# Attention with joined tanh and joined exponentials, ahead of a gated and a three-branch feed-forward, on one core

## The chip, the cores and the metric

The kernel runs on one core of a Trainium2 chip. The metric is the device time of one execution in microseconds (us). The engines are named as the profile names them: PE multiplies matrices (PEld is its loading of weights, which overlaps), ACT is ScalarE, DVE VectorE, POOL GpSimd, and SP issues the DMAs. SBUF is the on-chip memory of 128 partitions; PSUM has eight banks of 512 float32 columns per partition, into which PE writes.

## The reference, cut to what matters

Three stages follow each other; all inputs and outputs are float32.

```python
# q, k, v: (2, 12, 448, 64); cap = 30
scores = (q @ k.T) / sqrt(64)
scores = cap * tanh(scores / cap)
attn   = softmax(scores)            # guard 1e-9 in the sum
x      = (attn @ v) as (896, 768)

h = x @ w_in                        # 768 -> 2048
g = P(h) / (Q(h) + 1e-6)            # P cubic, Q = 1 + |b0||h| + |b1|h^2
x = g @ w_out                       # 2048 -> 768

h = max(x @ w1, x @ w2, x @ w3)     # 768 -> 768 each
out = h @ w_out2                    # 768 -> 768
```

## The kernel before, in words

**Attention.** The 24 heads of the two batches are 12 pairs of heads, and two pairs make a group `d` (six groups, `B * ND`). The 448 keys are three chunks of 128 (`NFULL` = 3) and a short rest of 64. `scores(d, i)` (line 566) makes one score value of a group: for i from 0 to 5, pair `r = i // 3` and chunk `n = i % 3`, and for i = 6 the rests of both pairs. Such a value is 128 keys by 448 queries for two heads and takes two PSUM banks, one per head (`singles`, line 334; `pair`, line 358). On it run
- PE: `products` (line 578, four instructions; mode "rows") or `ends` (line 585, eight; mode "both"),
- ACT: `soft` (line 599), one tanh of 448 columns per head out of its bank, with `1/(8 cap)` as a scale in a one-column tensor,
- ACT: `expo` (line 602), one exponential over the 896 columns of both heads in SBUF, in place, with `cap` as a scale. The reference's maximum is not subtracted: the scores are bounded by `cap`.

The result `E[d, i]` lies in a slot of its own. `weighted_rest(d)` (line 619) multiplies the rest's exponentials with v, and `weighted(d, r)` (line 638, twelve instructions) those of the three chunks of a pair, two times six halves, into a bank. The softmax's sums come from `summed(d)`: for the first three groups (`ADDED`) DVE or POOL add the three chunks of a pair first (line 660), and PE then sums over the keys with ones (line 684, 16 instructions); for the last three groups PE sums all chunks (32 instructions). The sums go out of their bank (line 695) through DRAM for reshaping and reciprocals and return as rows that scale the product (`scale_pair`, line 714), which is then split into a high and a low part (lines 730 and 734).

**Weights.** They come as float64 bits into three `raw` buffers and are decoded to float32 by ACT or POOL and DVE (lines 419 to 442) and split into a high and a low part (lines 459 and 462); a weight takes a slot while it is decoded and two for its parts. This goes on beside attention. The feed-forward stages then run on PE without a pause: `up` (line 754), `down` (line 861), the products of the three branches by a 2x2 scheme with seven products (line 998), and `output` (line 1106).

**What sets the order.** No engine's order is written out. Each operation is entered by `add` with its cost per engine that can run it, what it follows, and what memory it holds. `Flow.issue` (line 170) then plays the program through time, operation by operation: PE's operations carry due times from the order in which the program enters them, the others get theirs from those that need them, and each engine takes the earliest due that is ready and finds its memory. Costs of all engines but PE and SP are multiplied by `SPARE` (line 47, 1.08), and PE pays `SWITCH` for a change of mode (line 46). Operations marked `shared` go to whichever engine is free sooner by the plan. What the plan puts on an engine stays in that order on the chip.

**Memory.** 51 slots (`NSLOT`) of 2 x 448 columns hold everything in SBUF except constants, `raw` buffers and rows. `place` (line 113) gives a score value one of the pairs of banks (0, 1), (2, 3) and, for the first five groups (`EARLY`), also (6, 7): the pair that has been free the longest. As long as scores are to come, sums and products of attention use banks 4 and 5; after the last score all eight banks serve every kind.

Of the kernel before, what the change touches and what calls it, by code (L numbers as in the profile page):

```python
# [8 lines left out]
F32 = mybir.dt.float32  # L9
# [20 lines left out]
CAP = 6  # L30
NG = 6
LAG = 3
NSLOT, NRAW, NROW = 51, 3, 4
ND = NPAIR // 2
NFULL = S // P
WARM = 3
# [7 lines left out]
BACKLOG = 14.0, 2.0  # L44

SWITCH, SAME = {"rows": 0.21, "both": 0.16, "halves": 0.16, "quarters": 0.13, None: 0.2}, 6.0
SPARE = 1.08

MM, MO, FULL = 0.206, 0.1733, 0.752

# [29 lines left out]
class Flow:  # L80
# [6 lines left out]
    def __init__(self, pools, make):  # L87
        self.make = make
        self.ops, self.clock, self.free = [], 0.0, {k: list(range(n)) for k, n in pools.items()}
        self.banks, self.freed, self.log = [None] * 8, [0.0] * 8, []  # L90
        self.idle, self.t = {}, 0.0

    def add(self, engines, fn, after=(), vals=(), shared=False, due=None, leave=0, ahead=1e9, size=0.0, mode=None):
        first = next(iter(engines))
# [75 lines left out]
    def issue(self):  # L170
# [6 lines left out]
            assert op.due is not None, op.fn  # L177
        order = [op for op in ops if "pe" in op.engines]
        self.scores = sum(any(v.kind == "sc" for v in op.vals) for op in order)
        names = ("pe", "act", "dve", "pool", "sp")  # L180
        busy = dict.fromkeys(names, 0.0)
        current = dict.fromkeys(names)
# [8 lines left out]
        while left:  # L191
# [81 lines left out]
            while events and events[0][0] <= t + 1e-9:  # L273
                _, _, op = heapq.heappop(events)
                if op is None:
                    continue
                for v in op.vals:
                    v.users -= 1
                    if not v.users:
                        if v.kind in self.free:  # L280
                            self.free[v.kind].append(v.at[0])
                            if v.kind == "raw":
                                self.idle[v.at[0]] = t
                                seq += 1
                                heapq.heappush(events, (t + REST, seq, None))
                        else:
                            for i in v.at:
                                self.banks[i], self.freed[i] = None, t
                if any(v.kind == "sc" for v in op.vals) and "pe" in op.engines:
                    self.scores -= 1  # L290
                for s in op.next:
                    s.left -= 1
                    s.ready = max(s.ready, op.done + self.CROSS)
                    if not s.left:
                        k = len(ready)
                        while k and ready[k - 1].due > s.due:
                            k -= 1
                        ready.insert(k, s)
                        if s.ready > t:
                            seq += 1  # L300
                            heapq.heappush(events, (s.ready, seq, None))
# [8 lines left out]
def attention_moe(ctx: ExitStack, tc: tile.TileContext, qk, v, w_in, w_out, w123, w_out2, par, out):  # L310
# [6 lines left out]
    def open_pool(name, **kw):  # L317
        return ctx.enter_context(tc.tile_pool(name=name, bufs=1, reuse_waits="tile", **kw))

    cp = open_pool("consts")  # L320
    sp = open_pool("slots")
    pp = open_pool("banks", space=PSUM)
    dr = ctx.enter_context(tc.tile_pool(name="scratch", bufs=1, space=DRAM))


# [5 lines left out]
    ones = cp.tile([P, 3, Q], F32, name="ones")  # L331
    raws = [sp.tile([P, DM, 2], I32, name=f"raw{i}") for i in range(NRAW)]
    rows = [sp.tile([P, S], F32, name=f"row{i}") for i in range(NROW)]
    singles = [pp.tile([P, 512], F32, name=f"b{i}") for i in range(8)]
    a0, a1, a2, a3 = (con[:, i : i + 1] for i in range(4))
    b0, b1 = absb[:, 0:1], absb[:, 1:2]
    cap = con[:, CAP : CAP + 1]

    def make(val):
        if val.kind == "s":  # L340
            val.tile = sp.tile([P, 2, S], val.dt, tag=f"s{val.at[0]}", bufs=1, name=val.name)

    fl = Flow({"s": NSLOT, "raw": NRAW, "row": NROW}, make)
    add = fl.add

    def slot(name, dt=F32):
# [9 lines left out]
        return singles[val.at[0]]  # L356

    def pair(val, j):
        return singles[val.at[j]]

    def dma(out_, in_, after=(), vals=(), size=0.0, issue=0.4, **kw):
        return add({"sp": issue}, lambda e: nc.sync.dma_start(out=out_(), in_=in_()), after, vals, size=size, **kw)
# [197 lines left out]
        at = 2 * S - 2 * D + j * D  # L560
        return flat(vr, 2 * S)[r * D : r * D + D, at : at + D]

    last_tanh, last_copy = [], []


    def scores(d, i):
        whole_ = i < 2 * NFULL
        r, n = divmod(i, NFULL)
        pis = [2 * d + r] if whole_ else [2 * d, 2 * d + 1]
        t, x = Val("sc", f"sc{d}_{i}"), slot(f"e{d}_{i}")  # L570
        t.early = d < EARLY

        def products(e):
            raw = QK[pis[0]][0]
            q, k = two(raw)[:, 0], two(raw)[:, 1, n * P : n * P + P]
            for j in range(2):
                rr = slice(j * D, j * D + D)
                pe.matmul(pair(t, j)[:, :S], k[rr], q[rr], start=True, stop=True)  # L578

        def ends(e):  # L580
            for h, pi in enumerate(pis):
                raw = QK[pi][0]
                for j in range(2):
                    rr = slice(j * D, j * D + D)
                    pe.matmul(
                        pair(t, j)[h * D : h * D + D, :S], two(raw)[rr, 1, NFULL * P :], two(raw)[rr, 0],
                        start=True, stop=True,
                    )

        done = add(  # L590
            {"pe": FULL}, products if whole_ else ends, [QK[pi][1] for pi in pis], [QK[pi][0] for pi in pis] + [t],
            mode="rows" if whole_ else "both",
        )
        for th in last_tanh[-2:]:
            th.before(done)

        def soft(e):
            for j in range(2):
                act.activation(two(x)[:, j], pair(t, j)[:, :S], AF.Tanh, scale=qscale)  # L599

        def expo(e):
            act.activation(two(x), two(x), AF.Exp, scale=cap)  # L602

        th = add({"act": 1.03}, soft, [done, scale_in], [t, x])
        last_tanh.append(th)
        E[d, i] = x, add({"act": 0.935}, expo, [th], [x])

    AV, XU = {}, {}

# [1 line left out]
    def weighted_rest(d):  # L611
        vr, got_v = VV[d]
        o = [Val("av", f"av{d}_{r}") for r in range(2)]
        x, ex = E[d, 2 * NFULL]

        def products(e):
            for r in range(2):
                for j in range(2):
                    pe.matmul(  # L619
                        bank(o[r])[j * D : j * D + D, :S], rest(vr, r, j), two(x)[r * D : r * D + D, j],  # L620
                        start=True, stop=False,
                    )

        done = add({"pe": FULL}, products, [ex, got_v], [*o, x, vr], mode="both")
        AV[d] = o, done
        XU[d] = slot(f"xu{d}"), []
        for c in last_copy[-2:]:
            c.before(done)

    def weighted(d, r):  # L630
        vr, got_v = VV[d]
        o, dep = AV[d][0][r], AV[d][1]
        es = [E[d, r * NFULL + n] for n in range(NFULL)]

        def products(e):
            for n, (x, _) in enumerate(es):
                for j in range(2):
                    pe.matmul(  # L638
                        bank(o)[j * D : j * D + D, :S], whole(vr, n, r, j), two(x)[:, j], start=False,
                        stop=n == NFULL - 1,  # L640
                    )

        dep = add(
            {"pe": NFULL * FULL}, products, [got_v, dep] + [ex for _, ex in es], [o, vr] + [x for x, _ in es],
            mode="halves",
        )
        xu, parts = XU[d]
        parts.append(add(
            {"dve": 0.54, "act": 0.43}, lambda e: copy_on[e](two(xu)[:, r], bank(o)[:, :S]), [dep], [o, xu]
        ))  # L650
# [3 lines left out]
    def added(d, r):  # L654
        y, done = slot(f"es{d}_{r}"), None
        for n in range(ADDED[d]):
            (x, ex), (z, ez) = (E[d, r * NFULL] if n == 0 else (y, done)), E[d, r * NFULL + n + 1]

            def plus(e, x=x, z=z):
                engine[e].tensor_tensor(out=two(y), in0=two(x), in1=two(z), op=ALU.add)  # L660

            done = add({"dve": 1.0, "pool": 2.1}, plus, [ex, ez, done], [x, y, z], shared=True)
        ADDS[d, r] = y, done

    def summed(d):
        if ADDED[d]:
# [11 lines left out]
        def products(e):  # L678
            for n in range(last + 1):
                for r in range(2):  # L680
                    x = rounds[r][n][0]
                    for j in range(2):
                        g = (2 * r + j) * Q
                        pe.matmul(  # L684
                            bank(t)[g : g + Q, :S], ones[:, 0 if n < last else 1 + r], two(x)[:, j], start=n == 0,
                            stop=n == last, tile_position=(0, g),
                        )

        es = rounds[0] + rounds[1]
        dep = add(  # L690
            {"pe": (last + 1) * FULL}, products, [ex for _, ex in es] + [filled], [t] + [x for x, _ in es],
            mode="quarters",
        )
        got = add(
# [486 lines left out]
```

## Time and profile before

| | |
|---|---|
| median of the timed runs | 495.18 us (three runs, 495.1 to 497.91) |
| the profiled execution | 500.3 us |
| its span, first to last instruction | 498.5 us |
| PE busy | 492.1 us, 99% |
| DVE busy | 425.6 us, 85% |
| ACT busy | 335.5 us, 67% |
| POOL busy | 93.4 us, 19% |
| tanh, line 599 | 84 instructions of 128x448 |
| exponential, line 602 | 42 instructions of 128x896 |

All numbers of the trace are from the one profiled execution. Busy time of PE counts pipelined matrix multiplications with modelled ends, so a full PE row does not by itself mean that PE never waited; starts of instructions and the list of waits tell that.

### The profile page before, as it was taken

To read this page: it belongs to the slowest core of one execution; us is meant where nothing else is said; L and a number is where in the kernel's file an instruction comes from. 1 tells how busy PE (TensorE), PEld (TensorE's weight loads), DVE (VectorE), ACT (ScalarE), POOL (GpSimd) and SP (SyncE) were. 2 spreads that over 40 slices of the span, in tenths; PEclk is the share of its full clock that TensorE was granted. 3 is DMA by queue.
4 is the path that set the end of the run, shared out by engine and by line. 5 is a ranking of instruction groups with operands and counts; after the bars stand their busy time and mean duration, and the time that the engine had idled before them with its cause. 6 is when DMAs were issued, how large, how long until landed. Compare 5 with 4: busy or idle time off the path is not lost.

```text
span 498.5 us, 6724 instructions
## 1 busy us (share of the span) xinstructions
PE 492.1 (99%) x2508; PEld 400.8 (80%) x2508; DVE 425.6 (85%) x605; ACT 335.5 (67%) x443; POOL 93.4 (19%) x78
## 2 busy tenths in 40 slices
PE   8999999999999999999999999999999999999997
PEld 4432333479899999999999999999999999999996
DVE  0499999899999989989999999789999999989200
ACT  4999999978768878876586856574625454663211
POOL 0222223113311030220001000152223213102000
PEclk9999999999999999999999999999999999999999
DMA  7956545655000010311112576403235043220211
GB/s 285 411 201 240 165 156 158 221 143 188 2 0 1 0 64 1 126 65 63 65 42 85 192 252 215 165 0 128 83 114 183 2 141 111 84 107 1 96 64 63
DMA packets 16448, 58.36 MB, mean 117 GB/s; under 512 B 3592, under 2 KB 6944, under 8 KB 16416
## 3 DMA queue, kind: packets, MB, share of 16 engines
q1 hardware_dynamic: 16416, 57.94, 33.4%
q8 instruction: 19, 0.31, 0.3%
q14 instruction: 13, 0.11, 0.1%
HBM read 55.10 MB, written 2.84 MB: 116 GB/s over the span
## 4 chain that ended last, share of the span: by engine, by line
PE 86%; DVE 5%; ACT 4%; DMA 2%; issue 1%; SPq 0%; DVEq 0%
PE b L861 24%; PE b L998 24%; PE b L754 19%; PE b L1106 9%; PE b L578 4%; PE b L638 4%; PE b L684 3%; ACT e L599 2%; DVE es L660 2%; DMA raw<-in_w_out_dram 2%; DMA qk<-in_qk_dram 1%; PE b L619 1%; DVE decin L442 1%; DVE decin L423 1%; ACT e L602 1%
## 5 line engine op out<-in xcount | busy, mean ns | idle before, releaser
L754 PE MATMUL b<-x,whin 128*128 128x448 f32 x384 | 109.7, 367 | 0.0
L754 PEld LDWEIGHTS b<-x,whin 128*128 128x128 f32 x384 | 71.8, 188 | 8.3 <-issue 2.1
L754 PE MATMUL b<-x,wlin 128*128 128x448 f32 x192 | 70.1, 365 | 0.0
L998 PE MATMUL b<-T,mh 128*128 128x448 f32 x216 | 62.0, 368 | 0.0
L439 ACT ACTIVATE raw<-raw 128x768 uint8<-128x768 uint8 x30 | 58.1, 1974 | 0.1
L599 ACT ACTIVATE e<-b,qscale 128x448 f32<-128x448 f32 x84 | 47.7, 732 | 3.8 <-PE b L578 3.7
L998 PEld LDWEIGHTS b<-T,mh 128*128 128x128 f32 x216 | 40.5, 188 | 4.0
L602 ACT ACTIVATE e<-e,con 128x896 f32<-128x896 f32 x42 | 43.4, 1158 | 0.0
L998 PE MATMUL b<-T,ml 128*128 128x448 f32 x108 | 39.7, 368 | 0.0
L793 POOL TENSOR_TENSOR T<-T,A 128x448 f32<-128x448 f32 x16 | 23.9, 1493 | 82.6 <-ACT T L778 61.1
L754 PEld LDWEIGHTS b<-x,wlin 128*128 128x128 f32 x192 | 36.1, 188 | 2.9
L578 PE MATMUL b<-qk 64*128 64x448 f32 x144 | 36.5, 604 | 0.7 <-DMA qk<-in_qk_dram 0.7
L774 ACT ACTIVATE W<-b,con 128x448 f32<-128x448 f32 x32 | 23.1, 723 | 19.2 <-PE b L754 19.1
L861 PE MATMUL b<-gl,whoa 128*128 128x448 f32 x96 | 35.2, 367 | 0.5 <-DVE gl L836 0.5
L861 PE MATMUL b<-gh,whob 128*128 128x448 f32 x96 | 35.3, 368 | 0.0
L861 PE MATMUL b<-gl,whob 128*128 128x448 f32 x96 | 35.3, 368 | 0.0
L861 PE MATMUL b<-gh,wlob 128*128 128x448 f32 x96 | 35.3, 368 | 0.0
L861 PE MATMUL b<-gh,wloa 128*128 128x448 f32 x96 | 35.1, 365 | 0.0
L861 PE MATMUL b<-gh,whoa 128*128 128x448 f32 x96 | 35.1, 365 | 0.0
L419 POOL TENSOR_SCALAR decin<-raw 128x768 f32<-128x768 f32 x15 | 19.0, 1267 | 80.5 <-DMA raw<-in_w_in_dram 38.1
L578 PEld LDWEIGHTS b<-qk 64*128 64x128 f32 x144 | 15.7, 197 | 20.2 <-ACT e L599 9.7
L998 PE MATMUL b<-B,mh 128*128 128x448 f32 x108 | 31.0, 368 | 0.0
(157 smaller groups left out, 1132.3 us busy)
## 6 DMA issues: line engine op xcount, KB each, us to landing
raw<-in_w_out_dram SPq DMA_DIRECT2D x22, 768.0 KB, 4.2
raw<-in_w_dram SPq DMA_DIRECT2D x18, 768.0 KB, 4.3
raw<-in_w_in_dram SPq DMA_DIRECT2D x16, 768.0 KB, 5.1
qk<-in_qk_dram SPq DMA_DIRECT2D x12, 448.0 KB, 7.4
v<-in_v_dram SPq DMA_DIRECT2D x6, 448.0 KB, 6.0
row<-rsum SPq DMA_DIRECT2D x24, 112.0 KB, 2.9
out_dram<-ob SPq DMA_DIRECT2D x6, 384.0 KB, 2.7
out_dram<-ob SPq DMA_DIRECT2D x2, 192.0 KB, 1.9
```

The lines of the kernel that those rows point to most:

```text
L419: engine[e].tensor_scalar(out=o, in0=i, scalar1=2.0**-112, scalar2=0.0, op0=ALU.mult, op1=ALU.add)
L439: act.activation(byte[:, 4::8], byte[:, 3::8], AF.Copy, scale=1 / 32, bias=-31 / 64)
L578: pe.matmul(pair(t, j)[:, :S], k[rr], q[rr], start=True, stop=True)
L599: act.activation(two(x)[:, j], pair(t, j)[:, :S], AF.Tanh, scale=qscale)
L602: act.activation(two(x), two(x), AF.Exp, scale=cap)
L638: pe.matmul(bank(o)[j * D : j * D + D, :S], whole(vr, n, r, j), two(x)[:, j], start=False, stop=n == NFULL - 1,)
L754: pe.matmul(bank(h)[:, :S], w_, x_, start=cc == 0 and i == 0, stop=cc == NCC - 1 and i == len(terms) - 1)
L774: act.activation(two(w_)[:, i], bank(h)[:, :S], AF.Identity, bias=a2, scale=a3)
L793: engine[e].tensor_tensor(out=two(t_)[:, i], in0=two(t_)[:, i], in1=two(a_)[:, i], op=ALU.mult)
L861: pe.matmul(bank(a)[:, :S], w_, g_, start=count[half, o, b] == 1, stop=count[half, o, b] == 3 * NFC)
L998: pe.matmul(bank(o)[:, :S], w_, m_, start=cc == 0 and i == 0, stop=cc == 2 and i == 2)
L1106: pe.matmul(bank(o)[:, :NH], h_, w_, start=ocs[0] == 0 and i == 0, stop=ocs[-1] == NCC - 1 and i == len(terms) - 1,)
```

## The change

Banks 0 to 3 become two tiles of two banks each (`twins`) as long as scores are to come. A score value that lies in one of them gets its tanh by one instruction over both banks; one in banks 6 and 7 still takes two. The three chunks of a pair of heads share one tile of SBUF, a triple (`tri`, four of them, `NTRI`, kind "t"), and one exponential over its 2688 columns follows the third tanh. The rest of the keys keeps a slot and an exponential of its own. Twelve of the 51 slots are held back for the triples and return to the slots when the last triple is released; the two pools are closed at that point and at the first later use of a bank below 4, and pools for single slots and banks are opened in their place. In the plan, a tanh in a two-bank tile costs 0.89 and any other 1.03, the long exponential 0.187 + 3 x 0.747, and `SPARE` is 1.06.

```diff
-NSLOT, NRAW, NROW = 51, 3, 4
+NSLOT, NRAW, NROW, NTRI = 51, 3, 4, 4
...
-SPARE = 1.08
+SPARE = 1.06
+
+TANH = 0.89
...
         self.idle, self.t = {}, 0.0
+        self.held = 3 * pools["t"]
+        self.late, self.free["s"] = self.free["s"][len(self.free["s"]) - self.held :], self.free["s"][: -self.held]
...
                             self.free[v.kind].append(v.at[0])
+                            if v.kind == "t":
+                                self.triples -= 1
+                                if not self.triples:
+                                    self.free["s"] += self.late
...
-    singles = [pp.tile([P, 512], F32, name=f"b{i}") for i in range(8)]
+    singles = [None] * 4 + [pp.tile([P, 512], F32, name=f"b{i}") for i in range(4, 8)]
+    tri = triples_open.enter_context(tc.tile_pool(name="triples", bufs=1, reuse_waits="tile"))
+    pairs = pairs_open.enter_context(tc.tile_pool(name="pairs", bufs=1, reuse_waits="tile", space=PSUM))
+    twins = [pairs.tile([P, 2, 512], F32, name=f"bb{i}") for i in range(2)]
...
     def make(val):
+        at = val.at[0]
+        if val.kind == "t":
+            val.tile = tri.tile([P, NFULL, 2, S], val.dt, tag=f"t{at}", bufs=1, name=val.name)
         if val.kind == "s":
-            val.tile = sp.tile([P, 2, S], val.dt, tag=f"s{val.at[0]}", bufs=1, name=val.name)
+            if at >= NSLOT - 3 * NTRI and not late:
+                triples_open.close()
+                late.append(open_pool("late"))
+            pool = late[0] if at >= NSLOT - 3 * NTRI else sp
+            val.tile = pool.tile([P, 2, S], val.dt, tag=f"s{at}", bufs=1, name=val.name)
+        if val.kind in ("h", "acc", "av") and at < 4 and singles[0] is None:
+            pairs_open.close()
+            more = open_pool("more", space=PSUM)
+            singles[:4] = [more.tile([P, 512], F32, name=f"b{i}") for i in range(4)]
...
     def pair(val, j):
-        return singles[val.at[j]]
+        at = val.at[j]
+        return twins[at // 2][:, at % 2] if at < 4 else singles[at]
...
-        t, x = Val("sc", f"sc{d}_{i}"), slot(f"e{d}_{i}")
+        t = Val("sc", f"sc{d}_{i}")
         t.early = d < EARLY
+        if not whole_:
+            x = slot(f"e{d}_{i}")
+            view = lambda: two(x)
+        else:
+            if not n:
+                TRI[d, r] = Val("t", f"e{d}_{r}"), []
+            x, parts = TRI[d, r]
+            view = lambda: x.tile[:, n]
...
         def soft(e):
+            if t.at[0] < 4:
+                act.activation(view(), twins[t.at[0] // 2][:, :, :S], AF.Tanh, scale=qscale)
+                return
             for j in range(2):
-                act.activation(two(x)[:, j], pair(t, j)[:, :S], AF.Tanh, scale=qscale)
+                act.activation(view()[:, j], pair(t, j)[:, :S], AF.Tanh, scale=qscale)
 
         def expo(e):
-            act.activation(two(x), two(x), AF.Exp, scale=cap)
+            all_ = two(x) if not whole_ else x.tile.rearrange("p n j s -> p (n j s)")
+            act.activation(all_, all_, AF.Exp, scale=cap)
 
-        th = add({"act": 1.03}, soft, [done, scale_in], [t, x])
+        th = add({"act": TANH}, soft, [done, scale_in], [t, x])
         last_tanh.append(th)
-        E[d, i] = x, add({"act": 0.935}, expo, [th], [x])
+        if not whole_:
+            E[d, i] = x, add({"act": 0.935}, expo, [th], [x]), view
+            return
+        parts.append(th)
+        if n == NFULL - 1:
+            ex = add({"act": 0.187 + 0.747 * NFULL}, expo, parts, [x])
+            for k in range(NFULL):
+                E[d, r * NFULL + k] = x, ex, lambda k=k: x.tile[:, k]
```

The rest of the diff passes the views of `E` on to the products, additions and sums that read them, counts the triples, and sets the planned cost of a tanh by the banks that its score has got.

## Rows read from the trace of the kernel before

**Rows 1.** Waits of PE: who waited for whom, us in total, times, longest.

```profile
PE b L861 <- DVE gl L836: 0.5, 1, 0.5
PE b L684 <- DVE es L660: 0.4, 1, 0.4
```

**Rows 2.** Chain that ended last, from 46 us on: start us, us, what.

```profile
46.07 1.70 PE b L684 x12
47.77 2.46 PE b L578 x12
...
51.89 2.41 PE b L638 x12
54.29 1.70 PE b L578 x8
...
60.86 1.64 PE b L684 x16
...
87.39 3.14 PE b L684 x32
...
103.09 3.86 PE b L754 x18
```

**Rows 3.** Stretches: length, busy PE, PEld, DVE, ACT, POOL, clock, DMA, GB/s.

```profile
10.57:47.70 37.13, 36.68 (x195) 13.46 (x193) 28.43 (x34) 37.02 (x59) 9.27 (x8) 1.00 0.80 307
47.70:103.02 55.32, 55.32 (x350) 21.00 (x348) 53.83 (x85) 52.82 (x76) 14.40 (x10) 1.00 0.52 166
103.02:131.01 27.99, 27.52 (x136) 24.83 (x134) 25.83 (x38) 22.23 (x30) 5.53 (x5) 1.00 0.41 131
```

**Rows 4.** Timeline of PE, 12 to 45 us: start us, us, engine, line, what.

```profile
12.27 7.99 PE L578 MATMUL b<-qk 64*128 64x448 f32 x32
20.19 0.98 PE L619 MATMUL b<-e,v 64*64 64x448 f32 x8
...
27.07 2.81 PE L638 MATMUL b<-e,v 128*64 128x448 f32 x12
29.81 3.27 PE L578 MATMUL b<-qk 64*128 64x448 f32 x12
33.01 0.96 PE L684 MATMUL b<-es,ones 128*32 128x448 f32 x8
...
36.35 1.72 PE L619 MATMUL b<-e,v 64*64 64x448 f32 x8
38.00 2.48 PE L638 MATMUL b<-e,v 128*64 128x448 f32 x12
...
44.68 0.95 PE L684 MATMUL b<-es,ones 128*32 128x448 f32 x4
```

**Rows 5.** Timeline of PE's weight loads, with the idle time before and its releaser.

```profile
37.10 0.20 PEld L619 LDWEIGHTS b<-e,v 64*64 64x64 f32 x4 [0.56 <-DVE row L695]
```

**Rows 6.** Timeline of ACT, 7 to 32 us.

```profile
7.69 1.16 ACT L599 ACTIVATE e<-b,qscale 128x448 f32<-128x448 f32 x2 [2.99 <-PE b L578]
...
10.68 8.52 ACT L599 ACTIVATE e<-b,qscale 128x448 f32<-128x448 f32 x16 [0.33 <-PE b L578]
18.97 1.15 ACT L602 ACTIVATE e<-e,con 128x896 f32<-128x896 f32 x1
19.90 2.33 ACT L599 ACTIVATE e<-b,qscale 128x448 f32<-128x448 f32 x4
...
28.60 3.40 ACT L599 ACTIVATE e<-b,qscale 128x448 f32<-128x448 f32 x6
```

**Rows 7.** Groups of ACT by line and shape: count, busy us, mean ns of one.

```profile
L459 ACT CAST mh<-decm 128x768 fp32r<-128x768 f32 x15 | 12.6, 840 | 8.0 <-DVE decm L432 4.6 <-PE b L998 2.2 <-DVE decm L490 1.1
...
L459 ACT CAST mx<-decm 128x384 fp32r<-128x384 f32 x9 | 4.7, 523 | 10.9 <-DVE decm L490 3.9 <-PE b L998 3.3 <-DVE ml L462 2.8
```

**Rows 8.** Groups of DVE by line, operations on a weight.

```profile
L462 DVE TENSOR_TENSOR wlin<-decin,whin 128x768 fp32r<-128x768 f32 x16 | 16.2, 1014 | 0.0
L432 DVE SCALAR_TENSOR_TENSOR decin<-raw,decin 128x768 int32<-128x768 int32 x16 | 15.9, 996 | 0.3
```

More of the change, by code (lines that the diff above doesn't have):

```diff
@@ L179, in issue @@
         self.scores = sum(any(v.kind == "sc" for v in op.vals) for op in order)
+        self.triples = len({id(v) for op in ops for v in op.vals if v.kind == "t"})
         names = ("pe", "act", "dve", "pool", "sp")
@@ L322, in attention_moe @@
     pp = open_pool("banks", space=PSUM)
+    pairs_open, triples_open = ExitStack(), ExitStack()
+    ctx.enter_context(triples_open)
+    ctx.enter_context(pairs_open)
     dr = ctx.enter_context(tc.tile_pool(name="scratch", bufs=1, space=DRAM))
@@ L337, in attention_moe @@
     cap = con[:, CAP : CAP + 1]
+    late = []
     def make(val):
+        at = val.at[0]
+        if val.kind == "t":
+            val.tile = tri.tile([P, NFULL, 2, S], val.dt, tag=f"t{at}", bufs=1, name=val.name)
         if val.kind == "s":
-            val.tile = sp.tile([P, 2, S], val.dt, tag=f"s{val.at[0]}", bufs=1, name=val.name)
-    fl = Flow({"s": NSLOT, "raw": NRAW, "row": NROW}, make)
+            if at >= NSLOT - 3 * NTRI and not late:
[7 more added lines that the diff above has]
+            singles[:4] = [more.tile([P, 512], F32, name=f"b{i}") for i in range(4)]
+    fl = Flow({"s": NSLOT, "raw": NRAW, "row": NROW, "t": NTRI}, make)
     add = fl.add
@@ L561, in rest @@
         return flat(vr, 2 * S)[r * D : r * D + D, at : at + D]
-    last_tanh, last_copy = [], []
+    last_tanh, last_copy, TRI = [], [], {}
     def scores(d, i):
@@ L575, in products @@
             q, k = two(raw)[:, 0], two(raw)[:, 1, n * P : n * P + P]
+            th.engines["act"] = (TANH if t.at[0] < 4 else 1.03) * SPARE
             for j in range(2):
@@ L580, in ends @@
         def ends(e):
+            th.engines["act"] = (TANH if t.at[0] < 4 else 1.03) * SPARE
             for h, pi in enumerate(pis):
@@ L613, in weighted_rest @@
         o = [Val("av", f"av{d}_{r}") for r in range(2)]
-        x, ex = E[d, 2 * NFULL]
+        x, ex, view = E[d, 2 * NFULL]
         def products(e):
@@ L619, in products @@
                     pe.matmul(
-                        bank(o[r])[j * D : j * D + D, :S], rest(vr, r, j), two(x)[r * D : r * D + D, j],
+                        bank(o[r])[j * D : j * D + D, :S], rest(vr, r, j), view()[r * D : r * D + D, j],
                         start=True, stop=False,
@@ L635, in products @@
         def products(e):
-            for n, (x, _) in enumerate(es):
+            for n, (_, _, view) in enumerate(es):
                 for j in range(2):
                     pe.matmul(
-                        bank(o)[j * D : j * D + D, :S], whole(vr, n, r, j), two(x)[:, j], start=False,
+                        bank(o)[j * D : j * D + D, :S], whole(vr, n, r, j), view()[:, j], start=False,
                         stop=n == NFULL - 1,
@@ L643, in weighted @@
         dep = add(
-            {"pe": NFULL * FULL}, products, [got_v, dep] + [ex for _, ex in es], [o, vr] + [x for x, _ in es],
+            {"pe": NFULL * FULL}, products, [got_v, dep] + [ex for _, ex, _ in es], [o, vr] + [x for x, _, _ in es],
             mode="halves",
@@ L656, in added, with plus @@
         for n in range(ADDED[d]):
-            (x, ex), (z, ez) = (E[d, r * NFULL] if n == 0 else (y, done)), E[d, r * NFULL + n + 1]
-            def plus(e, x=x, z=z):
-                engine[e].tensor_tensor(out=two(y), in0=two(x), in1=two(z), op=ALU.add)
+            (x, ex, one), (z, ez, other) = (E[d, r * NFULL] if n == 0 else (y, done, lambda: two(y))), E[d, r * NFULL + n + 1]
+            def plus(e, one=one, other=other):
+                engine[e].tensor_tensor(out=two(y), in0=one(), in1=other(), op=ALU.add)
             done = add({"dve": 1.0, "pool": 2.1}, plus, [ex, ez, done], [x, y, z], shared=True)
-        ADDS[d, r] = y, done
+        ADDS[d, r] = y, done, lambda: two(y)
     def summed(d):
@@ L680, in products @@
                 for r in range(2):
-                    x = rounds[r][n][0]
+                    x = rounds[r][n][2]()
                     for j in range(2):
@@ L684, in products @@
                         pe.matmul(
-                            bank(t)[g : g + Q, :S], ones[:, 0 if n < last else 1 + r], two(x)[:, j], start=n == 0,
+                            bank(t)[g : g + Q, :S], ones[:, 0 if n < last else 1 + r], x[:, j], start=n == 0,
                             stop=n == last, tile_position=(0, g),
@@ L690, in summed @@
         dep = add(
-            {"pe": (last + 1) * FULL}, products, [ex for _, ex in es] + [filled], [t] + [x for x, _ in es],
+            {"pe": (last + 1) * FULL}, products, [ex for _, ex, _ in es] + [filled], [t] + [x for x, _, _ in es],
             mode="quarters",
```

## The prediction

> **What bounds the kernel now.** I read four views in this order. First the list of waits of the matrix engine (PE): behind 47.7 us of the span it holds one wait, 0.5 us [rows 1]. So the later 450 us are PE work without a hole, and what the change can give back has to be found ahead of that point. Second, the chain that ended last: from 46.07 to 106.95 us it is 30 PE pieces, each beginning where the one before it ends [rows 2]. From the same rows come the full-rate prices: three score operations (x12) take 2.46 us and two (x8) 1.70, so one costs 0.76 and the change of mode about 0.2; a weighted product (x12) costs 2.41 and a row sum of the first kind (x16) 1.64. Third, the engines by stretch: from 10.57 to 47.7 us ScalarE (ACT) is busy 37.02 of 37.13 us, while VectorE (DVE) is busy 28.43; from 47.7 to 103.02 us ACT, DVE and PE are all nearly full (52.82, 53.83 and 55.32 of 55.32) [rows 3]. Early on ACT sets the pace, later PE does, with DVE close behind it.
>
> Fourth, PE's timeline of the early stretch gives the idle time by subtraction [rows 4]:
> - 12.27 to 20.19 us: eight scores take 7.92; at full rate 8 x 0.76 + 0.2 = 6.28. Idle 1.64; ACT's tanh paces them.
> - 20.19 to 29.81 us: two operations on the short rest of the keys, then a score and a weighted product twice, take 9.62; at full rate, with 0.16 for a change of mode, 2 x 0.92 + 2 x (0.92 + 2.41) = 8.50. Idle 1.12; the products follow the exponentials.
> - 29.81 to 33.01 us: three scores take 3.20 against 2.46. Idle 0.74; tanh again.
> - 36.35 to 38.00 us: one product of the short rest takes 1.65 against 0.92. Idle 0.73; it waits for DVE's copy of a row sum out of its bank [rows 5].
> - 44.68 to 47.77 us: a row sum takes 3.09 against 1.64. Idle 1.45; it waits for DVE's additions (the second wait in rows 1).
>
> Together 5.68 us: 3.50 behind ACT and 2.18 behind DVE. Whatever ACT saves, the end can move by little more than this.
>
> **The change, part by part.**
>
> *One tanh over two banks.* Sixteen single tanhs run from 10.68 to 18.97 us [rows 6], 0.518 us each, and two are a score's: 1.036. No row shows one instruction that reads two banks. What an ACT element costs comes from two casts: 840 ns for 768 columns, 523 for 384 [rows 7], so 317 / 384 = 0.826 ns a column and 0.370 us for 448. That leaves 0.148 us fixed per tanh, which the joined one pays once: 0.888 us, 0.148 saved. The other end comes from the kernel's own pair: tanh on 448 columns 0.518, exponential on 896 0.93 (18.97 to 19.90) [rows 6], or 0.92 ns a column and 0.106 fixed, 0.106 saved. Lowest of all, crossing from bank to bank eats the whole saving: 0. A loss is left out, because the same columns are read with one start fewer. I take 0.148, since the two casts differ in size alone. A score lies in banks 0 to 3 in two of three cases for the first five groups of heads (35 scores, three pairs of banks) and always in the last group (7 scores): about 23 + 7 = 30. Saved: 30 x 0.148 = 4.4 us of ACT.
>
> *One exponential for three chunks.* An exponential costs 0.93, of which 2 x 0.370 = 0.740 are columns and 0.19 fixed. Three in one: 0.19 + 3 x 0.740 = 2.41 against 2.79, so 0.38 saved, twelve times: 4.6 us. With 0.106 fixed it is 0.21 x 12 = 2.5. Both parts: 9.0 us of ACT, at the low end 2.5 (no gain from the joined tanh).
>
> The Trainium skill, ScalarE: Activation LUTs, section on the ACT_TABLE_LOAD cost ("What ACT_TABLE_LOAD costs"), gives an ACTIVATE with one pointer operand about 280 ns plus 0.833 ns a column, with an overlap of about 93 ns back to back. By that an estimate for the single tanh is 0.56 us, which the trace has at 0.518, and for the exponential 0.93, which the trace has too. It would make the saving of a joined tanh 0.19 instead of 0.148 and ACT's total about 10 us instead of 9.0.
>
> *What of it reaches the end.* By 28.60 us ACT has done 26 tanhs (13 scores, some 8.7 of them joined) and two triples of exponentials [rows 6]: 8.7 x 0.148 + 2 x 0.38 = 2.05 us ahead. Against it stands a loss. Now a weighted product runs behind its exponentials chunk by chunk: the second one starts at 27.07, before the third exponential ends at 28.60, and PE goes on at 29.81, 1.21 us after that end. With one exponential it can start only at its end and needs 2.41: 1.20 us of overlap gone. Net at 29.81: 2.05 - 1.20 = 0.85 us. The three scores behind it then find their banks emptied and run in 2.46 instead of 3.20: 0.74 more, 1.6 us at 33.01. The loss of overlap does not return: from 38.00 us on the weighted products run at full rate (x12 in 2.41), their exponentials done before. At 44.68 ACT is further ahead (23 scores, four triples: 15.3 x 0.148 + 4 x 0.38 = 3.8 us), so DVE's additions get their inputs earlier, but DVE's own queue stands between. Of the 2.18 us behind DVE I take 0.9: at worst none goes, at best all. Sum: 1.6 + 0.9 = 2.5 us. With ACT's savings at their low end the first part is 2 x 0.21 - 1.20 + 0.74 = 0, and with some of the second about 0.5 remain.
>
> *After 47.7 us* ACT's remaining 5 us of savings lie beside full PE work and move nothing. They cover something else, though: PE now comes 2.5 us earlier to everything, and DVE has 1.5 us free until 103.02 and 2.2 until 131.01 [rows 3]. The planner lets ACT take over casts and copies where DVE is behind, and I cost this at nothing on that cover. Without it, PE's lead would be paid back, up to 2.5 us.
>
> *Tiles and planner.* Four triples hold 12 of the 51 slots all through attention, where before each chunk took its slot and gave it back alone. Two groups of heads need all four triples, so the next group's first tanh waits until the oldest group's weighted products and additions, and from the fourth group on its row sum, are done. In the program's order these stand ahead of the next group's scores, so I cost this at nothing, with ACT's lead as cover; the upper bound is a row sum, 1.64 or 3.14 us [rows 2], for each of the four groups to which it can happen. Closing the pools issues no work; the first users of banks 0 to 3 wait for the last joined tanh as before for the last single one. SPARE 1.06 for 1.08 and the new costs reorder everything that is planned by time; with about 0.2 us for each change of PE's mode [rows 2], five more or fewer are 1 us either way.
>
> The profiled execution took 500.3 us, its span 498.5; the median of the timed runs is 495.18. The 2.5 us are taken off both: 497.8 for a profiled run, 492.7 for the median.
>
> **The rivals.**
> 1. *DVE holds the pace, nothing comes.* The joined operations close later and may come too late for DVE's additions; or the two-bank tanh saves nothing, so that the change does not do what it says. Then the 0.5 us of the low end remain at most: 494.7 to 495.2. For it: DVE ends the last early wait. Against it: 3.50 of the 5.68 us are behind ACT.
> 2. *All early idle goes.* Order and inputs fall so that neither ACT nor DVE keeps PE waiting: 495.18 - 5.7 = 489.5. For it: ACT's lead of 3.8 us by then; against it: the 1.20 us of lost overlap and DVE's queue.
> 3. *Slower: the slots that the triples keep.* Two triples fall idle when the fifth group's row sum ends (about 90.5 us), but their six slots go to nobody until the last weighted product ends at 103.09 [rows 2]. That is room for two decoded weights (three slots each). Of each, DVE does two operations of 0.996 us (one has a row, the other the same shape) and one of 1.014 [rows 8], 3.0 us, so 6.0 us of DVE work slip to a time when 2.2 us are free until 131 us. 6.0 - 2.2 = 3.8 us, and PE's lead of 2.5 us makes them come later still in its own time: 6.3 late, 495.18 - 2.5 + 6.3 = 499.0. It decides from the point at which more than 4.7 us (2.2 and the lead) slip. For it: DVE is 97% busy there. Against it: no wait in the trace names a lack of room, and ACT gets spare time in just this stretch.
>
> **How the numbers follow.** Forecast, 1 to 4.5 us gained: 0.60. Rival 1, within 1 us: 0.17. Rival 2, more than 4.5: 0.11. Rival 3 and other disorder from the new plan, slower: 0.12. The range reaches to rival 2 with a us for fewer mode changes (488.5) and to near rival 3 (498.0). 1% is 4.95 us, about what a measurement of this kernel can tell from no change: over it on the fast side lies most of rival 2 and a little of the forecast's upper end, 0.13; on the slow side the worse half of rival 3, 0.07; between, 0.80.
>
> **What would show it.** Right: tanhs of 896 columns at 0.89 us from start to start, some 30 of them; twelve exponentials of 2688 columns at 2.4; ACT's attention ends some 9 us earlier or has other work between; PE's idle time ahead of its unbroken run is about 3 us instead of 5.7, and that run begins correspondingly earlier. Wrong: PE waits of over 1 us behind 50 us of the span, on decoded weights or on DVE (rival 3); the row sums of the first groups still waiting for DVE's additions at the same time as before (rival 1); a joined tanh at 1.03 us.

## The result and the profile after

The changed kernel takes 492.08 us in the median of 20 runs, against 496.0 us for the kernel before in 20 runs beside it: a ratio of 0.9917, with a 95% interval of 0.9896 to 0.9938, so some 4 us faster (3 to 5). The forecast was 492.7 us.

The profile on which the prediction rests comes from one of the longer executions (nine of the 20 runs before took 497 us or more, one of the 20 after 494 us or more; the fastest are 494.70 and 491.62 us), in which PE ran its first scores at half rate and its products from about 280 us on 2% slower, so a second profile of the same kernel (run before_again) is the one to compare with here. First lines of the two pages, after and before:

```profile
span 490.4 us, 6637 instructions
PE 482.6 (98%) x2508; PEld 399.1 (81%) x2508; DVE 415.2 (85%) x596; ACT 337.2 (69%) x402; POOL 91.8 (19%) x73
```

```profile
span 492.7 us, 6724 instructions
PE 487.0 (99%) x2508; PEld 400.3 (81%) x2508; DVE 425.9 (86%) x605; ACT 335.0 (68%) x443; POOL 96.2 (20%) x78
```

The spans differ by 2.3 us, a little less than the medians. ACT has 41 instructions less, yet no less busy time: it took over work from DVE and POOL. What the joined instructions cost is in ACT's groups, after and then before_again (count, busy us, mean ns of one); line 638 is the joined tanh, 641 the single one, 645 the exponential:

```profile
L638 ACT ACTIVATE e<-bb,qscale 128x896 f32<-128x896 f32 x31 | 31.4, 1069 | 3.4 <-PE bb L616 3.0 <-PE b L734 0.5
L645 ACT ACTIVATE e<-e,con 128x2688 f32<-128x2688 f32 x12 | 31.3, 2608 | 0.1
...
L641 ACT ACTIVATE e<-b,qscale 128x448 f32<-128x448 f32 x22 | 13.5, 705 | 0.0
...
L645 ACT ACTIVATE e<-e,con 128x896 f32<-128x896 f32 x6 | 6.9, 1146 | 0.0
```

```profile
L599 ACT ACTIVATE e<-b,qscale 128x448 f32<-128x448 f32 x84 | 47.7, 748 | 2.4 <-PE b L578 2.4
L602 ACT ACTIVATE e<-e,con 128x896 f32<-128x896 f32 x42 | 43.7, 1171 | 0.0
```

Before they are 91.4 us together, after 83.1: 8.3 us saved of the 9.0 forecast, with 31 joined tanhs for the 30 expected. From start to start a joined tanh takes 0.89 us and a long exponential 2.43 (19.77 to 22.20), as ACT's timeline after shows. The separate last line is from before_again and is the tanh that follows the second pair's three exponentials there:

```profile
9.00 1.92 ACT L638 ACTIVATE e<-bb,qscale 128x896 f32<-128x896 f32 x2
10.78 1.19 ACT L641 ACTIVATE e<-b,qscale 128x448 f32<-128x448 f32 x2
...
19.77 2.62 ACT L645 ACTIVATE e<-e,con 128x2688 f32<-128x2688 f32 x1
22.20 1.99 ACT L638 ACTIVATE e<-bb,qscale 128x896 f32<-128x896 f32 x2
```

```profile
26.14 3.44 ACT L599 ACTIVATE e<-b,qscale 128x448 f32<-128x448 f32 x6
```

Where the time came from stands in PE's timeline. First after (line 616 scores, 688 weighted products, 734 row sums), then before_again, which answers to [rows 4]; both begin their first score at 5.1 us:

```profile
5.11 1.77 PE L616 MATMUL bb<-qk 64*128 64x448 f32 x8
...
18.22 2.48 PE L688 MATMUL b<-e,v 128*64 128x448 f32 x12 [1.45 <-ACT e L645]
...
24.85 1.77 PE L616 MATMUL bb<-qk 64*128 64x448 f32 x8
...
28.07 0.96 PE L734 MATMUL b<-es,ones 128*32 128x448 f32 x8
...
30.44 1.02 PE L616 MATMUL bb<-qk 64*128 64x448 f32 x4 [0.66 <-ACT e L638]
31.39 1.38 PE L669 MATMUL b<-e,v 64*64 64x448 f32 x6
...
40.94 0.96 PE L734 MATMUL b<-es,ones 128*32 128x448 f32 x8
...
42.59 1.78 PE L616 MATMUL bb<-qk 64*128 64x448 f32 x8
```

```profile
5.09 2.53 PE L578 MATMUL b<-qk 64*128 64x448 f32 x12
...
27.38 3.27 PE L578 MATMUL b<-qk 64*128 64x448 f32 x12
30.58 0.96 PE L684 MATMUL b<-es,ones 128*32 128x448 f32 x8
...
32.22 1.77 PE L578 MATMUL b<-qk 64*128 64x448 f32 x8
...
42.55 0.94 PE L684 MATMUL b<-es,ones 128*32 128x448 f32 x4
43.96 0.57 PE L684 MATMUL b<-es,ones 128*32 128x448 f32 x2 [0.46 <-DVE es L660]
...
45.58 0.65 PE L578 MATMUL b<-qk 64*128 64x448 f32 x2
```

An instruction that begins earlier is a gain only if PE has done the same work by then, and the order has changed. Behind the second weighted product PE goes on at 24.85 instead of 27.38 us (2.53 earlier), but with 11 scores done for 13; the first row sum begins at 28.07 instead of 30.58 (2.51 earlier), with 15 scores for 16. At three points the two kernels have done exactly the same operations. Counted from each kernel's first score (5.09 and 5.11 us), in us:

| PE has done | before_again | after | gained |
|---|---|---|---|
| 16 scores and the first row sum (at 32.22 and 31.39) | 27.13 | 26.28 | 0.85 |
| 19 scores, all else up to the second row sum (42.55, 40.94) | 37.46 | 35.83 | 1.63 |
| the second row sum as well (45.58, 42.59) | 40.49 | 37.48 | 3.01 |

Between the last two points lie 1.65 us for 3.03 before: the wait for DVE's additions is gone. So 3.0 us are gained at 43 us, and 2.3 are left at the end of the span. PE's waits after, all of them:

```profile
PE b L688 <- ACT e L645: 1.4, 1, 1.4
PE b L428 <- DVE idle L396: 1.4, 1, 1.4
PE bb L616 <- ACT e L638: 0.7, 1, 0.7
PE b L804 <- DVE W L838: 0.2, 1, 0.2
PE b L911 <- DVE gl L886: 0.2, 1, 0.2
```

The first is the closing wait that the long exponential adds ahead of the first weighted product; the two of 0.2 us are the only ones behind 31 us. DVE, in the stretch that was 97% full before, has become freer (after, columns as in [rows 3]): 50.17 of 55.00 us, where before_again has 55.26 of 55.50 between 45.5 and 101 us.

```profile
41.00:96.00 55.00, 55.00 (x358) 21.17 (x358) 50.17 (x81) 51.34 (x52) 8.38 (x7) 1.00 0.48 166
```

### The profile page after: what moved, and what is told of

Its sections match the earlier page's. It is cut to its first block, busy times and chain, and to the rows that moved or that the text cites. A ratio compares the mean times of both kernels' runs of the same rounds, so it can differ in the third digit from the quotient of the medians.

```text
span 490.4 us, 6637 instructions
## 1 busy us (share of the span) xinstructions
PE 482.6 (98%) x2508; PEld 399.1 (81%) x2508; DVE 415.2 (85%) x596; ACT 337.2 (69%) x402; POOL 91.8 (19%) x73
## 4 chain that ended last, share of the span: by engine, by line
PE 84%; ACT 6%; DVE 5%; DMA 3%; issue 1%; SPq 0%; DVEq 0%; ACTq 0%
PE b L1048 23%; PE b L911 22%; PE b L804 17%; PE b L1156 9%; PE b L688 4%; PE bb L616 3%; PE b L734 3%; ACT e L638 2%; ACT e L645 2%; PE b L669 1%; DMA rsum<-comp 1%; ACT e L641 1%; DMA row<-rsum 1%; DMA qk<-in_qk_dram 1%; PE b L616 1%
## 5 line engine op out<-in xcount | busy, mean ns | idle before, releaser
L468 ACT ACTIVATE raw<-raw 128x768 uint8<-128x768 uint8 x31 | 60.1, 1984 | 0.1
L645 ACT ACTIVATE e<-e,con 128x2688 f32<-128x2688 f32 (+1 forms) x18 | 37.5, 2120 | 0.1
L638 ACT ACTIVATE e<-bb,qscale 128x896 f32<-128x896 f32 x31 | 31.4, 1069 | 3.4 <-PE bb L616 3.0
L688 PE MATMUL b<-e,v 128*64 128x448 f32 x144 | 28.8, 545 | 1.5 <-ACT e L645 1.4
L843 POOL TENSOR_TENSOR T<-T,A 128x448 f32<-128x448 f32 x10 | 13.4, 1340 | 81.0 <-ACT T L828 67.3
L1156 PE MATMUL b<-who,h3h 128*128 128x384 f32 x84 | 28.1, 335 | 0.0
L1156 PE MATMUL b<-who,h3l 128*128 128x384 f32 x84 | 28.1, 335 | 0.0
L1156 PE MATMUL b<-wlo,h3h 128*128 128x384 f32 x84 | 28.1, 335 | 0.0
```

The costliest lines, as they stand in the source:

```text
L468: act.activation(byte[:, 4::8], byte[:, 3::8], AF.Copy, scale=1 / 32, bias=-31 / 64)
L638: act.activation(view(), twins[t.at[0] // 2][:, :, :S], AF.Tanh, scale=qscale)
L645: act.activation(all_, all_, AF.Exp, scale=cap)
L688: pe.matmul(bank(o)[j * D : j * D + D, :S], whole(vr, n, r, j), view()[:, j], start=False, stop=n == NFULL - 1,)
L843: engine[e].tensor_tensor(out=two(t_)[:, i], in0=two(t_)[:, i], in1=two(a_)[:, i], op=ALU.mult)
L1156: pe.matmul(bank(o)[:, :NH], h_, w_, start=ocs[0] == 0 and i == 0, stop=ocs[-1] == NCC - 1 and i == len(terms) - 1,)
```

## The experiments

Theory A: the gain is ScalarE's saved time ahead of PE's unbroken run. Rival P: the gain is the new order that the planner drew. Others are named where they are tried. Medians below are over 4 to 12 runs, the kernel before beside them 495.7 us (497.1 in the last group); an interval is some 1 to 2.5 us to either side, so differences of 1.5 us and less between two variants are only indications.

**The order alone: before_spare106, after_spare108, after_spare107.**

```diff
-SPARE = 1.08
+SPARE = 1.06
```

> The kernel before with the plan's factor SPARE at 1.06 and nothing else of the change. Theory A (ScalarE's savings ahead of PE's unbroken run carry the gain): within 1.5 us of the kernel before, 494.5 to 497.5 us. Rival P (the new order that comes from the new factor carries it): 492 to 493 us, like the change.

Measured 503.45 us, ratio 1.015 (1.0119 to 1.0181). The same edit the other way round in the changed kernel:

> The changed kernel with SPARE back at 1.08. Theory A: 491.5 to 494 us, most of the gain stays. Rival P: 495 to 496 us, the gain is gone.

Measured 507.26 us, 1.0229 (1.0198 to 1.0259). Both theories missed both: the factor does not carry the gain, since alone it costs 8 us, and without it the joined instructions bring no gain either: that kernel is 12 us slower than the one before and 15 slower than the change. And half way:

> The changed kernel with SPARE 1.07, half way between the change (1.06) and the slow plan (1.08). If the factor acts as a margin that is too wide, the time lies between, 496 to 502 us. If it only redraws the order (rival P), it may be as fast as the change, and where it is slow the lost time stands as waits of PE behind 100 us and a granted clock below 1 after them, not ahead of 41 us.

Measured 498.68 us, 1.0051 (1.0021 to 1.0081). That number is in the range of a margin too wide; rival P forecast no number, only the place of the loss. Most of it is in the same place in all three runs. PE's waits behind 50 us in after_spare108, and two stretches of it (line 911 is `down`; the last number but two is the granted clock):

```profile
PE b L804 <- DVE W L838: 1.8, 2, 1.6
PE b L911 <- ACT whoa L488: 1.6, 1, 1.6
PE b L911 <- DVE gl L886: 1.5, 2, 1.1
PE b L1156 <- ACT who L488: 1.4, 1, 1.4
PE b L911 <- POOL wloa L491: 1.2, 1, 1.2
PE b L1156 <- DVE wlo L491: 0.8, 1, 0.8
```

```profile
265.00:270.00 5.00, 2.24 (x9) 1.32 (x9) 5.00 (x7) 2.48 (x4) 1.99 (x1) 1.00 0.45 157
270.00:275.00 5.00, 4.88 (x17) 4.02 (x15) 5.00 (x8) 2.76 (x2) 0.00 (x0) 0.66 0.00 0
```

PE starves behind the end of `up` (its last product begins at 258.33 us): split weights (`whoa`, `wloa`) and low parts of `g` (`gl`) come late, while DVE is busy 5.00 of 5.00 us, as it is in the change. After the waits the granted clock falls to a mean of 0.66, so that 17 products run in 5 us where the change runs 27. In after_spare107 the same place has 0.66 granted from 265 to 270 us and 3.94 us of PE in the next 5; before_spare106 has 0.70 from 275 to 280. By the products that are missing against the change (against before_again for before_spare106), at 0.20 us each, an estimate of the loss in these 10 to 15 us is 6.7 of the 14.0 us between the spans in after_spare108, 5.9 of 6.9 in after_spare107 and 5.7 of 7.5 in before_spare106; after_spare108 also waits 2.2 us for weights of `output` (line 1156). These waits stand behind 41 us, as the last expectation's second half said. Ahead of it the order of before_spare106 is even the better one, with the instructions of the kernel before:

```profile
5.54 2.53 PE L578 MATMUL b<-qk 64*128 64x448 f32 x12 [0.48 <-DMA qk<-in_qk_dram]
...
44.06 2.53 PE L578 MATMUL b<-qk 64*128 64x448 f32 x12
```

With the same work done as in the last line of the table above it is there 38.52 us after its first score, for 40.49 in before_again. An order alone can move the early part by 2 us.

**The joined instructions alone, in an unchanged order: split_tanh, split_exp, split_both.** The plan keeps the costs of the change, so the order of every engine stays; only what ScalarE is given differs.

```diff
-            if t.at[0] < 4:
+            if t.at[0] < 4 and not (True):
                 act.activation(view(), twins[t.at[0] // 2][:, :, :S], AF.Tanh, scale=qscale)
```

> The changed kernel, planned with the same costs and so in the same order, but each tanh over two banks is issued as two of 448 columns. 16 of the 31 joined ones lie ahead of PE's unbroken run, which begins near 41 us; 16 x 0.146 = 2.3 us more ScalarE time there. Theory A: slower than the change by 1.5 to 2.5 us (493.6 to 494.6). Rival P: within 0.5 us of the change, because the order is the same.

Measured 493.55 us, 0.9955 of before (0.9936 to 0.9974): 1.5 us slower than the change, at the lower edge of A and outside P. Its profile's span is 491.9 us, 1.5 above.

```diff
         def expo(e):
+            if whole_ and (True):
+                for k in range(NFULL):
+                    act.activation(x.tile[:, k], x.tile[:, k], AF.Exp, scale=cap)
+                return
```

> The changed kernel, same plan and order, but each exponential over three chunks is issued as three. Four of the twelve lie ahead of PE's unbroken run: 4 x 0.38 = 1.5 us more ScalarE time there, against which the first weighted product can follow its exponentials again and its 1.4 us wait shrinks. Theory A: between 0.5 us faster and 1.0 us slower than the change (491.6 to 493.1). Rival B (the long exponential is where the gain comes from): slower by 1.5 to 2.5 us (493.6 to 494.6).

Measured 493.72 us, 0.9961 (0.9942 to 0.9981): 1.6 us slower than the change. A is missed, rival B holds: giving back the overlap does not pay for the longer exponentials.

> The changed kernel, same plan and order, with every joined tanh and every long exponential issued in its single parts, so that ScalarE runs the instructions of the kernel before. The two parts alone cost 1.5 and 1.6 us against the change. Theory A (ScalarE's saved time ahead of PE's unbroken run is the whole gain within this order): they add up, 494.7 to 495.8 us, the time of the kernel before. Rival S (the one saving hides behind the other, and the order brings the rest): 493.5 to 494.3 us.

Measured 497.38 us, 1.0032 (1.0011 to 1.0053): 5.3 us slower than the change and somewhat slower than the kernel before, beyond both ranges. More than the sum of the two (3.1): a reading, not shown by a run of its own, is that while one saving is left, it covers part of what the other lost. So within this order the whole gain at the end hangs on the joined instructions, and rival P is refuted as the source of the gain, though not as a condition for it.

This run also parts the early gain, because it has the order of the change and the instructions of before:

```profile
5.66 1.77 PE L616 MATMUL bb<-qk 64*128 64x448 f32 x8 [0.55 <-DMA qk<-in_qk_dram]
...
34.85 0.98 PE L673 MATMUL b<-e,v 64*64 64x448 f32 x8
...
43.63 0.96 PE L738 MATMUL b<-es,ones 128*32 128x448 f32 x8
44.41 0.93 PE L738 MATMUL b<-e,ones 128*32 128x448 f32 x8
45.66 2.07 PE L616 MATMUL bb<-qk 64*128 64x448 f32 x8 [0.31 <-ACT e L641]
```

At the three points of the table it is 29.19, 37.97 and 40.00 us behind its first score. By the end of the second row sum the joined instructions thus bring 2.5 us (40.00 to 37.48) and the order 0.5 (40.49 to 40.00). The wait for DVE's additions is gone here too, without ScalarE's saving and with PE only 0.5 us later at the sum: between 43.63 and 45.66 us PE waits 0.31 us, for a tanh. The new order by itself has the exponentials of the fourth triple done 2.1 us sooner (32.74 us after the first score for 34.83 in before_again; 29.38 in the change). And of the 5.2 us between this span (495.6) and that of the change, 0.55 are a first score that its input let begin later, 2.5 arise by 43 us, and the other 2.1 behind it.

**Early or late: split_first2, split_last4.** The same edits with `d < 2` and with `d >= 2` for `True`.

> The changed kernel, same plan and order, single parts in the first two groups of heads only, whose scalar work lies mostly ahead of 41 us. Theory A: most of the loss of both splits, 494.2 to 495.4 us. Rival L (ScalarE's savings count wherever they fall, because they free ScalarE for VectorE's work): a third of the loss, 492.8 to 493.5 us.

> The changed kernel, same plan and order, single parts in the last four groups of heads only. Theory A: behind 41 us the matrix engine is full, so nearly nothing is lost, 491.8 to 492.9 us. Rival L: two thirds of the loss, 493.7 to 494.6 us.

Measured 494.33 us (0.9982, 0.9958 to 1.0006) and 494.14 us (0.9968, 0.994 to 0.9996): 2.3 and 2.1 us slower than the change. The first is as A has it and not as L, the second as L has it and not as A: neither theory holds for both, and early and late splits cost about the same. The cut is not quite at 41 us, for five of the twenty tanhs that split_last4 splits run on ScalarE ahead of it (16 joined ones are there in the change, 11 of them in the first two groups). In the profile of split_last4 the first scores run at half rate as in the first profile of before (the first two take 3.14 us, for 1.60 in the change), so only the stretch behind its second row sum is read here. The beginnings of the second and third row sum, in split_first2 and then split_last4, with the third one of the change behind them:

```profile
43.29 0.96 PE L738 MATMUL b<-es,ones 128*32 128x448 f32 x8
...
57.27 0.96 PE L738 MATMUL b<-es,ones 128*32 128x448 f32 x8
```

```profile
42.98 0.96 PE L738 MATMUL b<-es,ones 128*32 128x448 f32 x8
...
57.87 0.96 PE L738 MATMUL b<-es,ones 128*32 128x448 f32 x8
```

```profile
54.92 0.96 PE L734 MATMUL b<-es,ones 128*32 128x448 f32 x8
```

In the change 13.98 us lie between the two sums (54.92 - 40.94). In split_first2 the same 13.98, after a second sum that is 2.0 us late against its first score (37.83 from 5.46 us, for 35.83 from 5.11): the early loss stays, and nothing is added. In split_last4 it is 14.89, 0.9 us more, with a wait of PE for a single tanh among it (0.33 us at 52.05). In split_both, whose first scores ran at full rate, it is 15.27 (58.90 - 43.63). So single instructions cost PE time behind 43 us as well.

**The closing wait: split_exp0**, with `d == 0` for `True` in the exponential alone.

> The changed kernel, same plan and order, the exponential issued in three parts in the first group of heads only, where PE waited 1.4 us for the first long one. ScalarE pays 2 x 0.38 = 0.8 us, the first weighted product can start 1.2 us earlier. Theory A (what counts is when ScalarE is done with a pair, not how finely it hands over): 0.3 us faster to 0.8 us slower than the change, 491.8 to 492.9 us. Rival O (the lost overlap is a cost of its own): 0.7 us or more faster, 491.4 us or less.

Measured 492.68 us, 0.9923 (0.9892 to 0.9954): within A's range, not told apart from the change. PE's wait of 1.45 us ahead of the first weighted product is gone from the trace; two waits for tanhs, 1.5 us together, stand where the change has one of 0.7, and the span is 490.7 us. What the finer handing over gives, ScalarE's longer work takes back.

**Using the room on DVE: added_half, added_four.**

```diff
-ADDED = 2, 2, 2, 0, 0, 0
+ADDED = 2, 2, 2, 1, 0, 0
```

> The changed kernel with one addition of two chunks per pair moved from PE's row sum to VectorE for the fourth group of heads (ADDED 1 in place of 0): PE saves one of four rounds, 0.75 us, VectorE gets two additions, 2 us, in a stretch where it has 4.8 us free in 55. If the room is real: 491.0 to 491.8 us. If the order that comes out matters more (rival P): anywhere from 490 to 505 us, with PE waits of over 1 us between 100 and 275 us.

Measured 504.44 us, 1.0143 (1.0094 to 1.0191). With 2 in place of 1:

> The changed kernel with all additions of the fourth group of heads on VectorE (ADDED 2): PE saves 1.5 us, VectorE gets four additions, 4 us, of the 4.8 us free. If the room is real: 490.3 to 491.5 us. Rival P: 490 to 505 us, with PE waits of over 1 us between 100 and 275 us.

Measured 505.01 us, 1.0163 (1.0121 to 1.0206). Rival P both times, the second at the upper edge of its range: PE waits 2.3 us for one high part of `g` (DVE gh L883) and is busy 45.5 and 44.3 us of the 50 from 250 to 300 us, with 0.97 of the clock granted. What DVE's added 2 and 4 us of work cost of themselves, apart from the new order, no run separates. No version beat the change.

**A second profile of the kernel before: before_again.**

> The kernel before once more, for a second profile. If the first scores at half speed (5.8 to 9.7 us) and the 0.207 us between products from 280 us on belong to that one execution, the span is 493 to 494.5 us here, and the change's gain read from profiles is 3 to 4 us; if they belong to the kernel, the span is 498 to 499 us again and the gain read from profiles stays 8 us.

Measured one run of 494.49 us, span 492.7. Here the first weight loads of a score follow each other at half the distance (5.57, 5.95, 6.32 us for 6.70, 7.45, 8.20 in the first profile), and products from 300 to 350 us number 249 for 244. So both were of that execution, and 5.8 of the 8.1 us between the first two profiles are not the change's.

## Why the prediction was right, and which steps were not

- *What an instruction saves* was right: a joined tanh 0.89 us for 0.888, a long exponential 2.43 for 2.41, 31 for 30 joined. The two casts gave the better end of the bounds. An estimate by the Trainium skill's formula (ScalarE: Activation LUTs, section What ACT_TABLE_LOAD costs) gives 2.43 us for the long exponential, as the trace has it, and 0.93 for the joined tanh, for which the trace's 0.89 stands.
- *The first part, 1.6 us by 33 us,* was mis-sized: at equal work (16 scores and the first row sum) it is 0.85. Its mechanism is there. ScalarE saves 8 joined tanhs x 0.146 + 2 x 0.37 = 1.9 us by the end of the second pair's exponentials, for 2.05 forecast; the lost overlap is 1.41 us (24.85 - 22.20 = 2.65 from that end to PE's next work, for 27.38 - 26.14 = 1.24), for 1.20 forecast. The term that failed is the 0.74 us behind them: the scores do run at full rate, but the new plan put one of them behind the row sum, and PE waits 0.66 us for a tanh there. The exponentials end 3.94 us earlier (22.20 for 26.14); the other 2 us are two scores' tanhs put later, and they are no gain, since PE has two scores fewer done as well.
- *DVE's part, 0.9 of 2.18 us,* was mis-sized the other way, and its cause was not the one given. Between the first row sum and the end of the second 2.2 us are gained (3.01 - 0.85), 1.4 of them the whole wait for DVE's additions. The prediction had them come from ScalarE's lead; in split_both the wait is gone without that lead, so the new order removes it. Whether the lead alone would have done it in the old order, no run shows, and what brings the other 0.8 us is not separated.
- That 3.0 us stood at 43 us, for 2.5 forecast, is therefore in part luck: one term was 0.75 too large, the other 1.3 too small. The base was off as well: the forecast took its 2.5 us off 495.18 us, the median of three runs, and 20 runs have 496.0.
- *"After 47.7 us ACT's savings move nothing"* failed as a step. In the order of the change, single instructions in the later groups cost 0.9 us by the third row sum and 2.1 us in the end, by an interval that holds 1 to 4, and split_both loses 2.1 us behind 43 us. PE is without a wait there because ScalarE is quick enough; with a slower ScalarE it waits there.
- *The planner's reordering, "1 us either way",* is the step that was worst mis-sized. Mode changes were the wrong measure: an order moved the early part by 0.5 us (split_both) and 2 us (before_spare106), and it costs by PE starving near 270 us and by the clock after it, and four neighbouring plans of the changed kernel cost 6.6 to 15 us more than it does, one of the kernel before 7.8 us. The forecast held because this plan has no such place, which the profile of before could not show: that is luck, not foresight. Rival 3 had the right mechanism, late decoding on DVE, but looked for it before 131 us and in room that the triples keep; the chance of 0.12 for all disorder was thin.
- *DVE's cover* was real: ScalarE took over work (nine scalings of `w_in` weights for one), and DVE's busy time fell by 10.7 us. Rival 1 is out by the result, and rival 2 by PE's 1.4 and 0.7 us of waits that stayed.

## What to carry to other kernels

Work out a joined instruction from the same operation at two sizes, then ask at which engine's pace the stage runs: here 8.3 us of ScalarE time became 2.3 to 4 us of kernel. Where an order has changed, compare two timelines only at points where the same work is done: here an apparent gain of 2.5 us at 28 us was one of 0.85 at the next such point. Where a planner draws the order, a change of costs is two changes; run the new instructions in a fixed order (plan as changed, issue the parts) to read the one without the other. An order that fits is a result of its own: edits that would each save PE 0.75 or 1.5 us lost 12 to 13 us with the order redrawn.

## What the runs showed of the hardware that was not expected

One ScalarE instruction may read two PSUM banks at no visible price: 0.89 us for 896 columns from two banks (128x896, line 638), where one fixed part and the columns by the two casts make 0.888, and 0.93 for 896 columns of SBUF.

The granted clock does not tell all of PE's rate. In the first profile of before the scores from 5.8 to 9.7 us ran at half the rate of those in before_again, and from 300 to 350 us it made 244 products where before_again made 249, with 1.00 granted in both. The profile of split_last4 shows both again (243 products), that of added_half the second alone (243). Ahead of the slow first scores PE had waited 0.69 and 0.65 us for its first input; the cause is open.

In after_spare108 the granted clock did fall. The 0.66 above is the mean of two levels:

```profile
271.00:272.00 1.00, 1.00 (x4) 0.89 (x3) 1.00 (x3) 1.00 (x1) 0.00 (x0) 0.50 0.00 0
```

Behind PE's two waits of 1.6 and 1.2 us, from 270.5 to 273.9 us, the products came 0.37 us apart for 0.20, at the level of 1.2 GHz.
